# Block-sparse attention and a Fourier mixing layer: copies and the norm's root moved to GpSimd, attention prepared earlier

## The chip, the cores and the metric

The kernel runs on one core of one Trainium2 chip. The metric is the device time of one execution in microseconds (us), lower is better. The kernel is written in Python against the engines: TensorE (PE) for matrix products, VectorE (DVE), ScalarE (ACT), GpSimd (POOL) and SyncE (SP), which only issues DMAs here. Each engine works through its own list of instructions in order and waits at semaphores for the others. GpSimd also issues DMAs, those that convert float32 to float16 on the way.

## The reference

First attention with block selection: q, k, v have the shape (4 batches, 8 heads, 768 positions, 64), float32. Keys form 12 blocks of 64. A query scores each block by its product with the block's mean key, keeps the three best blocks that are not in its future, and its own block. Then the usual softmax attention with a causal mask over the kept blocks:

```python
scores = scale * np.matmul(q, k.transpose(0, 1, 3, 2))
mask = mask & (pos[:, None] >= pos[None, :])
scores = np.where(mask, scores, -1000000000.0)
...
return np.matmul(attn, v)
```

Its result is laid out as x of shape (4, 768, 512), and a Fourier mixing layer with a feed-forward follows:

```python
X = np.fft.fft(x, axis=1)
X = np.fft.fft(X, axis=2)
u = x + np.real(X)
mu = np.mean(u, axis=-1, keepdims=True)
var = np.mean((u - mu) ** 2, axis=-1, keepdims=True)
un = (u - mu) / np.sqrt(var + 1e-06)
out = u + np.maximum(un @ w_ch1, 0.0) @ w_ch2
```

w_ch1 is 512 x 2048, w_ch2 is 2048 x 512.

## The kernel before, in words

The unit of attention is a pair: two heads of one batch, 16 pairs in all, four per batch. A pair P goes through these stages:

- `load` (L160): k and q of both heads by SyncE into float32 tiles (three buffers each); v of pairs 0 to 5 by SyncE into a float32 tile and then a GpSimd cast into one of four float16 v buffers (L171); v of later pairs straight into that buffer by a GpSimd DMA (L164).
- `stage_A` (L186): TensorE transposes k and q into PSUM. VectorE sums k by block (L202) and copies q as float32 (L210). ScalarE copies k of both heads into `qk` (L205), and q of head 0 (L211); VectorE copies q of head 1 (L212).
- `stage_G` (L214): the block scores on TensorE (L220, L223), then on VectorE a transpose (L226), twelve instructions for the top entries (L229), a comparison and a product, and a transpose back into `mt`.
- `stage_K` (L238): GpSimd copies `mt` into the rows 64 to 95 of `qk`, four copies per pair (L241). The score product over 96 rows then adds the block mask by itself.
- `stage_S` (L246), in six parts: scores on TensorE (L260), exponential on ScalarE (L265), and the causal triangle by an `affine_select` on GpSimd (L268), which keeps an element where an affine function of its indices holds.
- `stage_V` (L271): probabilities times v on TensorE (L281), divided by their sum on VectorE into x.

A batch then goes through the mixing layer: folds of x on VectorE (`stage_fold`, `stage_fg`), the transform over positions as matrix products (`stage_Y`, L334, with PSUM copies on ScalarE, L347, and mirrored on VectorE, L349), the transform over features with the residual (`stage_M`, L354: three parts of two row blocks each), the norm in the same function, the feed-forward `stage_W1` (L406) and `stage_W2` (L422).

The norm in `stage_M`: VectorE adds x to the product (u), takes mean and variance (L377, L378), and computes 1/sqrt(var + 1e-6) from an integer seed and two Newton steps (L382 to L391), all as [128,2] instructions. One row block is then normalized on ScalarE (L397), the other on VectorE (L399), and SyncE issues one transposing DMA for each (L403). The feed-forward needs all six.

The order: `attn_slot(i, g, a)` (L483) gives a list of pieces that score pair i, gate pair g, finish pair i-1 and prepare pair a (and load k and q of pair a+3 behind it). Slots 0 to 4 run ahead of everything (L577 to L584). Then, for each batch, the rest of the attention and the batch's mixing layer are woven into one sequence by weights (`weave`, L532). A scheduler lays out each engine's list from that sequence, by its own estimate of when operands are ready; only SyncE's list is kept in exactly the order of the program.

Of the kernel before, what the change touches and what calls it, by code (L numbers as in the profile page):

```python
# [11 lines left out]
FP = mybir.dt.float32  # L12
# [7 lines left out]
S = 768  # L20
# [78 lines left out]
def kernel(  # L99
# [36 lines left out]
    def tt(out, in0, in1, op, eng=None):  # L136
        (eng or nc.vector).tensor_tensor(out=out, in0=in0, in1=in1, op=op)  # L137

    fs_sb = ctile([128, 2, 2, 3, KE], F16, "fs_sb")
    fd_sb = ctile([128, 6, 256], F16, "fd_sb")  # L140
    id32 = ctile([128, 128], FP, "id32")
# [18 lines left out]
    def load(P, who, eng):  # L160
        b, hp = divmod(P, NP)
        src = (q, k, v)[who]
        if who == 2 and P >= NHV:
            nc.gpsimd.dma_start(v_s[P % NVS][:, :, :, 0:64].rearrange("p e st d -> p (e st) d"),  # L164
                                src[b, 2 * hp:2 * hp + 2]
                                .rearrange("e (st p) d -> p (e st) d", p=128))
            return
        if who == 2:
            t = apool.tile([128, 2 * NST, 64], FP, tag="nat2", name=f"nat2_{P}", bufs=2)
            eng.dma_start(t, src[b, 2 * hp:2 * hp + 2].rearrange("e (st p) d -> p (e st) d", p=128))  # L170
            nc.gpsimd.tensor_copy(  # L171
                out=v_s[P % NVS][:, :, :, 0:64].rearrange("p e st d -> p (e st) d"), in_=t)
            return
        if P >= NPAIR:
            return
        t = apool.tile([128, NST, 2, 64], FP, tag=f"nat{who}", name=f"nat{who}_{P}", bufs=3)
        for e in range(2):
            eng.dma_start(t[:, :, e, :],
                          src[b, 2 * hp + e].rearrange("(st p) d -> p st d", p=128))
        nat[P, who] = t  # L180
# [5 lines left out]
    def stage_A(P):  # L186
        d = pairs[P]
        slot = P % NSLOT
        qk = qk_s[slot]
        q32 = apool.tile([128, S], FP, tag="q32", name=f"q32_{P}")  # L190
        d["q32"], d["slot"] = q32, slot
        for who in (1, 0):
            ps = pst([128, NST, 128], f"tp{who}_{P}")
            if 1 <= P <= 3:
                fill(ps.rearrange("p a c -> p (a c)"), 3)
            src = nat[P, who].rearrange("p st e d -> p st (e d)")
            for st in range(NST):
                nc.tensor.transpose(ps[:, st, :], src[:, st, :], id32)  # L198
            flat = ps.rearrange("p a c -> p (a c)")
            if who == 1:  # L200
                kr12 = spool.tile([128, NB], FP, tag="kr12", name=f"kr12_{P}")
                nc.vector.tensor_reduce(out=kr12, in_=flat.rearrange("p (n c) -> p n c", c=64),  # L202
                                        axis=mybir.AxisListType.X, op=ALU.add)
                for e in range(2):
                    nc.scalar.copy(out=qk[0:64, e, 1, :], in_=flat[64 * e:64 * e + 64])  # L205
                tt(kr_s[slot][:, :, 0:NB],
                   kr12.rearrange("p (o n) -> p o n", o=1).to_broadcast([128, 2, NB]), half,
                   ALU.mult)
            else:
                nc.vector.tensor_copy(out=q32, in_=flat)  # L210
                nc.scalar.copy(out=qk[0:64, 0, 0, :], in_=flat[0:64])  # L211
                nc.vector.tensor_copy(out=qk[0:64, 1, 0, :], in_=q32[64:128])  # L212

    def stage_G(P):  # L214
        d = pairs[P]
# [22 lines left out]
    def stage_K(P):  # L238
        mt = pairs[P]["mt"]
        for c in range(4):  # L240
            nc.gpsimd.tensor_copy(  # L241
                out=qk_s[P % NSLOT][64:96, :, 0, 192 * c:192 * c + 192],
                in_=mt[32 * c:32 * c + 32, :].rearrange("p (o x) -> p o x", o=1)
                .to_broadcast([32, 2, 192]))

    def stage_S(P, i):  # L246
        d = pairs[P]
# [106 lines left out]
    def stage_M(b, kp):  # L354
        u_b, x_b = bpool.tile([128, 2, DM], FP, tag="u_b", name=f"u{kp}_{b}", bufs=5), x_t[b]
        u_t[b, kp] = u_b
        mps = pst([128, 2, 512], f"mx{kp}_{b}")
        for k2 in range(2):
            kt = 2 * kp + k2
            sg = 0 if kt < 3 else 1  # L360
            rows = slice(128 * (kt % 3), 128 * (kt % 3 + 1))
            for par in range(2):
                src = ys[b, par][sg]
                o = mps[:, k2, 256 * par:256 * par + 256]
                nc.tensor.matmul(o, src[:, 0, rows], fd_sb[:, 3 * par, :], start=True, stop=False)
                nc.tensor.matmul(o, src[:, 1, rows], fd_sb[:, 3 * par + 1 + sg, :], start=False,
                                 stop=True)
        kk = slice(2 * kp, 2 * kp + 2)
        tt(u_b.rearrange("p k (m two) -> p k two m", two=2),
           mps.rearrange("p k (two m) -> p k two m", two=2),  # L370
           x_b[:, kk, :].rearrange("p k (m two) -> p k two m", two=2), ALU.add)
        if kp == 0:
            un_t[b] = bpool.tile([128, NDT, S], F16, tag="unT", name=f"unT_{b}", bufs=1)
        mv = spool.tile([128, 2, 2], FP, tag="mv", name=f"mv{kp}_{b}")
        for k2 in range(2):
            bst = spool.tile([128, 6], FP, tag="bst", name=f"bst{2 * kp + k2}_{b}", bufs=4)
            nc.vector.bn_stats(out=bst, in_=u_b[:, k2, :])  # L377
            nc.vector.bn_aggr(out=mv[:, k2, :], in_=bst)  # L378
        vr, t2, rs = [spool.tile([128, 2], FP, tag=n, name=f"{n}{kp}_{b}")
                      for n in ("vr", "t2", "rs")]  # L380
        yi = rs.bitcast(I32)
        nc.vector.tensor_scalar(out=vr, in0=mv[:, :, 1], scalar1=1e-6, scalar2=None, op0=ALU.add)  # L382
        nc.vector.tensor_scalar(out=yi, in0=vr.bitcast(I32), scalar1=1, scalar2=None,
                                op0=ALU.arith_shift_right)
        nc.vector.tensor_scalar(out=yi, in0=yi, scalar1=-1, scalar2=0x5f3759df,
                                op0=ALU.mult, op1=ALU.add)
        for _ in range(2):
            nc.vector.scalar_tensor_tensor(out=t2, in0=vr, scalar=-0.5, in1=rs,
                                           op0=ALU.mult, op1=ALU.mult)
            tt(t2, t2, rs, ALU.mult)  # L390
            nc.vector.scalar_tensor_tensor(out=rs, in0=t2, scalar=1.5, in1=rs,  # L391
                                           op0=ALU.add, op1=ALU.mult)
        nb = spool.tile([128, 1], FP, tag="nb", name=f"nb{kp}_{b}")
        nc.vector.tensor_scalar(out=nb, in0=mv[:, 0, 0:1], scalar1=rs[:, 0:1], scalar2=-1.0,  # L394
                                op0=ALU.mult, op1=ALU.mult)
        kt = 2 * kp
        nc.scalar.activation(out=x_b[:, kt, :], in_=u_b[:, 0, :], func=AF.Identity,  # L397
                             scale=rs[:, 0:1], bias=nb)
        nc.vector.tensor_scalar(out=x_b[:, kt + 1, :], in0=u_b[:, 1, :],  # L399
                                scalar1=mv[:, 1, 0:1], scalar2=rs[:, 1:2],  # L400
                                op0=ALU.subtract, op1=ALU.mult)
        for kt in range(2 * kp, 2 * kp + 2):
            nc.sync.dma_start_transpose(un_t[b][:, :, 128 * kt:128 * kt + 128], x_b[:, kt, :])  # L403

# [151 lines left out]
    with tc.manual_schedule(engines={mybir.EngineType.SP}):  # L556
        consts_first()
        kq(2)
        load(0, 2, nc.sync)
        load(1, 2, nc.sync)  # L560
        stage_A(0)
        stage_G(0)
        kq(3)
        stage_A(1)
        stage_K(0)
        stage_G(1)
        kq(4)
        stage_A(2)
        stage_K(1)
        load(2, 2, nc.sync)  # L570
        load(3, 2, nc.sync)
        nc.sync.dma_start(fs_sb, dr["FS"].ap())
        nc.sync.dma_start(fd_sb, dr["FD"].ap())
        for dt in range(NDT):
            load_w1(dt)
        kq(5)
        run(attn_slot(0, 2, 3))  # L577
        run(attn_slot(1, 3, 4))
        load(4, 2, nc.sync)
        run(attn_slot(2, 4, None))  # L580
        load(5, 2, nc.sync)
        run(attn_slot(3, None, 5))
        load(6, 2, nc.sync)
        run(attn_slot(4, 5, None))  # L584
        load(7, 2, nc.sync)
        for b in range(B):
            L = attn_slot(-9, None, 6) if b == 0 else []
            for i in range(NP * (b + 1) + 1, min(NP * (b + 2) + 1, NPAIR + 1)):
                L += attn_slot(i, i + 1, i + 2)
            weave(L, stream(b))  # L590


# [28 lines left out]
```

## Time and profile before

| | |
|---|---|
| median of 3 runs | 377.93 us |
| lowest and highest | 374.62 and 380.5 us |
| the profiled execution | 377.26 us |
| its span, first to last instruction | 375.4 us |
| mean granted TensorE clock | 0.923 of full |
| busy: TensorE, VectorE, ScalarE, GpSimd | 84%, 55%, 47%, 26% |

How to read it: a view of the profile gives an instruction as its start, its duration, its engine, the line of the kernel, what it writes and reads, and in square brackets how long the engine was idle before it and what ended that. "PE" is TensorE's matrix products; a "q" behind an engine's name means its queue (SPq: SyncE's). A clock of 1.00 is 2.4 GHz, 0.50 is 1.2 GHz.

### The profile page before, as it was taken

To read this page: it belongs to the slowest core of one execution; us is meant where nothing else is said; L and a number is where in the kernel's file an instruction comes from. 1 tells how busy PE (TensorE), PEld (TensorE's weight loads), DVE (VectorE), ACT (ScalarE), POOL (GpSimd) and SP (SyncE) were. 2 spreads that over 40 slices of the span, in tenths; PEclk is the share of its full clock that TensorE was granted. 3 is DMA by queue.
4 is the path that set the end of the run, shared out by engine and by line. 5 is a ranking of instruction groups with operands and counts; after the bars stand their busy time and mean duration, and the time that the engine had idled before them with its cause. 6 is when DMAs were issued, how large, how long until landed. Compare 5 with 4: busy or idle time off the path is not lost.

```text
span 375.4 us, 6443 instructions
## 1 busy us (share of the span) xinstructions
PE 316.5 (84%) x2478; PEld 184.6 (49%) x2478; DVE 205.7 (55%) x660; ACT 176.1 (47%) x214; POOL 97.7 (26%) x210
## 2 busy tenths in 40 slices
PE   7788975670599997987879999989999999499995
PEld 3455553350275654563536655653566455156542
DVE  1787678299065639499503738597423179512121
ACT  2478886345158655526546755325575220234200
POOL 3177961641042332311403132300311100000000
PEclk9899898596599999998969999998999999889999
DMA  9999999981615605431990303103300010420012
GB/s 177 211 212 269 201 216 191 210 85 28 141 10 98 87 20 78 86 22 28 141 217 2 21 2 28 50 3 68 130 0 2 2 56 2 84 112 2 0 56 112
DMA packets 94985, 32.45 MB, mean 86 GB/s; under 512 B 88812, under 2 KB 91052, under 8 KB 94956
## 3 DMA queue, kind: packets, MB, share of 16 engines
q1 hardware_dynamic: 74544, 24.98, 30.6%
q0 software_dynamic: 18400, 6.56, 15.7%
q10 hardware_dynamic: 2012, 0.52, 0.7%
q8 instruction: 19, 0.31, 0.3%
q14 instruction: 10, 0.08, 0.1%
HBM read 28.77 MB, written 6.29 MB: 93 GB/s over the span
## 4 chain that ended last, share of the span: by engine, by line
PE 54%; DVE 22%; ACT 10%; issue 5%; DMA 4%; SPq 1%; POOL 1%; ACTq 0%; POOLq 0%; DVEq 0%
PE c L429 15%; PE h L411 13%; PE h L413 7%; PE sc L260 6%; DVE u L137 5%; PE av L281 4%; DVE bst L377 3%; ACT qk L205 3%; ACT pt L265 3%; DMA unT<-x 3%; PE tp L198 2%; DVE kr L202 2%; PE g L220 2%; DMA nat<-in_q_dram 2%; DVE x L137 2%
## 5 line engine op out<-in xcount | busy, mean ns | idle before, releaser
L265 ACT ACTIVATE pt<-sc 128x1024 f16<-128x1024 f32 x96 | 84.6, 919 | 56.6 <-PE sc L260 56.2
L411 PE MATMUL h<-unT,w_sb 128*128 128x512 f16 x256 | 90.7, 398 | 17.4 <-DMA unT<-x 16.3
L429 PE MATMUL c<-w_sb,hT 128*128 128x512 f16 x384 | 89.0, 385 | 4.1 <-DVE x L137 2.1
L268 POOL TENSOR_SCALAR_AFFINE_SELECT pt<-pt 128x256 f16<-128x256 f16 x96 | 40.1, 426 | 149.8 <-ACT pt L265 148.8
L413 PE MATMUL h<-unT,w_sb 128*128 128x256 f16 x256 | 71.7, 283 | 6.7 <-DMA unT<-x 6.7
L420 ACT ACTIVATE hT<-h 128x768 f16<-128x768 f32 x48 | 38.7, 812 | 50.5 <-PE h L413 50.4
L260 PE MATMUL sc<-qk 96*128 96x512 f16 (+3 forms) x256 | 52.7, 316 | 10.3 <-POOL qk L241 3.1
L429 PEld LDWEIGHTS <-hT 128*128 128x128 f16 x384 | 37.5, 99 | 47.1 <-issue 7.7
L411 PEld LDWEIGHTS <-w_sb 128*128 128x128 f16 x256 | 25.8, 101 | 46.4 <-issue 22.5
L418 DVE TENSOR_SCALAR hT<-h 128x768 f16<-128x768 f32 x16 | 15.3, 956 | 59.8 <-PE h L413 59.8
L260 PEld LDWEIGHTS <-qk 96*128 96x128 f16 x256 | 24.0, 100 | 34.6 <-issue 15.1
L241 POOL COPY qk<-mt 32x384 f16<-32x384 f16 x64 | 33.0, 515 | 29.3 <-DVE mt L235 26.6
L205 ACT CAST qk<-tp 64x768 f16<-64x768 f32 x32 | 25.4, 794 | 26.2 <-DVE kr L202 26.0
L413 PEld LDWEIGHTS <-w_sb 128*128 128x128 f16 x256 | 25.9, 101 | 15.4 <-DMA unT<-x 9.2
L137 DVE TENSOR_TENSOR u<-c,u 128x1024 f32<-128x1024 f32 (+1 forms) x13 | 14.8, 1137 | 31.3 <-PE c L429 31.3
L198 PE MATMUL tp<-id,nat 128*128 128x128 f32 x192 | 26.1, 279 | 2.8 <-ACT pt L265 0.9
L281 PEld LDWEIGHTS <-pt 128*128 128x128 f16 x672 | 25.3, 98 | 3.8 <-POOL pt L268 0.8
L281 PE MATMUL av<-v,pt 128*128 128x65 f16 x672 | 26.9, 195 | 0.3 <-POOL pt L268 0.3
L198 PEld LDWEIGHTS tp<-id,nat 128*128 128x128 f32 x192 | 21.7, 143 | 6.8 <-issue 2.7
L226 DVE STREAM_TRANSPOSE gt<-g 128x192 f32<-128x192 f32 x16 | 6.1, 379 | 23.5 <-PE g L223 23.5
L397 ACT ACTIVATE x<-u,nb,rs 128x512 f16<-128x512 f32 x12 | 9.8, 814 | 18.9 <-DVE nb L394 18.9
L347 ACT CAST ty<-yp 128x772 f16<-128x772 f32 x8 | 8.3, 1033 | 19.1 <-PE yp L334 19.1
(73 smaller groups left out, 338.4 us busy)
## 6 DMA issues: line engine op xcount, KB each, us to landing
nat<-in_k_dram SPq DMA_DIRECT2D x32, 192.0 KB, 4.9
nat<-in_q_dram SPq DMA_DIRECT2D x30, 192.0 KB, 4.7
out_dram<-u SPq DMA_DIRECT2D x11, 512.0 KB, 3.0
w_sb<-in_moe_w_ch_dram POOLq DMA_DIRECT2D x8, 512.0 KB, 10.0
nat<-in_v_dram SPq DMA_DIRECT2D x6, 384.0 KB, 12.3
v<-in_v_dram POOLq DMA_DIRECT2D x10, 192.0 KB, 4.9
fs_sb<-c_FS SPq DMA_DIRECT2D x1, 582.0 KB, 5.9
out_dram<-u SPq DMA_DIRECT2D x2, 256.0 KB, 2.0
```

Of the source, the lines that this page charges most:

```text
L137: (eng or nc.vector).tensor_tensor(out=out, in0=in0, in1=in1, op=op)
L198: nc.tensor.transpose(ps[:, st, :], src[:, st, :], id32)
L205: nc.scalar.copy(out=qk[0:64, e, 1, :], in_=flat[64 * e:64 * e + 64])
L241: nc.gpsimd.tensor_copy(out=qk_s[P % NSLOT][64:96, :, 0, 192 * c:192 * c + 192], in_=mt[32 * c:32 * c + 32, :].rearrange("p (o x) -> p o x ...
L260: nc.tensor.matmul(ps[:, co:co + q1 - q0], qk[0:96, e, 1, 128 * jt:128 * jt + 128], qk[0:96, e, 0, q0:q1], start=True, stop=True)
L265: nc.scalar.activation(out=pt[:, o:o + wid], in_=ps, func=AF.Exp, scale=0.125)
L268: nc.gpsimd.affine_select(out=dg, in_=dg, pattern=[[0, 2], [1, 128]], base=0, channel_multiplier=-1, compare_op=ALU.is_ge, fill=0.0)
L281: nc.tensor.matmul(av[:, e, 66 * st:66 * st + 65], pt[:, co:co + 128], vv[:, e, jt, 0:65], start=(cnt == 0), stop=(cnt == 20))
L411: nc.tensor.matmul(hp[:, 0:512], w1s, unT[:, dt, 0:512], start=(dt == 0), stop=(dt == NDT - 1))
L413: nc.tensor.matmul(hp[:, 512:768], w1s, unT[:, dt, 512:768], start=(dt == 0), stop=(dt == NDT - 1))
L420: nc.scalar.activation(out=hT, in_=hp, func=AF.Relu)
L429: nc.tensor.matmul(cps[:, part, :], h_t[b, it][:, 128 * st:128 * (st + 1)], w2_sb[:, it, :], start=(it == 0), stop=(it == NIT - 1))
```

## The change

GpSimd gets a helper `pcopy`, an `affine_select` whose condition holds everywhere, so that it copies. It is used for v's casts, for the mask copies, and for the q copies of both heads, which read the float32 copy of q and leave ScalarE and VectorE. In the norm the seed stays on VectorE; the Newton steps and the bias go to GpSimd as ten [128,2] instructions, and both row blocks are normalized on ScalarE. In the order, pairs 5 and 6 are prepared and gated one slot earlier each, so that both are done ahead of the first FFT, and the first weave starts without pair 6.

```diff
+    def pcopy(out, in_, n):
+        nc.gpsimd.affine_select(out=out, in_=in_, pattern=[[0, i] for i in n], base=0,
+                                channel_multiplier=0, compare_op=ALU.is_ge, fill=0.0)
...
-            nc.gpsimd.tensor_copy(
-                out=v_s[P % NVS][:, :, :, 0:64].rearrange("p e st d -> p (e st) d"), in_=t)
+            pcopy(v_s[P % NVS][:, :, :, 0:64].rearrange("p e st d -> p (e st) d"), t,
+                  [2 * NST, 64])
...
                 nc.vector.tensor_copy(out=q32, in_=flat)
-                nc.scalar.copy(out=qk[0:64, 0, 0, :], in_=flat[0:64])
-                nc.vector.tensor_copy(out=qk[0:64, 1, 0, :], in_=q32[64:128])
+                for e in range(2):
+                    pcopy(qk[0:64, e, 0, :], q32[64 * e:64 * e + 64], [S])
...
         for c in range(4):
-            nc.gpsimd.tensor_copy(
-                out=qk_s[P % NSLOT][64:96, :, 0, 192 * c:192 * c + 192],
-                in_=mt[32 * c:32 * c + 32, :].rearrange("p (o x) -> p o x", o=1)
-                .to_broadcast([32, 2, 192]))
+            pcopy(qk_s[P % NSLOT][64:96, :, 0, 192 * c:192 * c + 192],
+                  mt[32 * c:32 * c + 32, :].rearrange("p (o x) -> p o x", o=1)
+                  .to_broadcast([32, 2, 192]), [2, 192])
...
+        nb = spool.tile([128, 2], FP, tag="nb", name=f"nb{kp}_{b}")
         yi = rs.bitcast(I32)
+        po = nc.gpsimd
...
         for _ in range(2):
-            nc.vector.scalar_tensor_tensor(out=t2, in0=vr, scalar=-0.5, in1=rs,
-                                           op0=ALU.mult, op1=ALU.mult)
-            tt(t2, t2, rs, ALU.mult)
-            nc.vector.scalar_tensor_tensor(out=rs, in0=t2, scalar=1.5, in1=rs,
-                                           op0=ALU.add, op1=ALU.mult)
-        nb = spool.tile([128, 1], FP, tag="nb", name=f"nb{kp}_{b}")
-        nc.vector.tensor_scalar(out=nb, in0=mv[:, 0, 0:1], scalar1=rs[:, 0:1], scalar2=-1.0,
-                                op0=ALU.mult, op1=ALU.mult)
-        kt = 2 * kp
-        nc.scalar.activation(out=x_b[:, kt, :], in_=u_b[:, 0, :], func=AF.Identity,
-                             scale=rs[:, 0:1], bias=nb)
-        nc.vector.tensor_scalar(out=x_b[:, kt + 1, :], in0=u_b[:, 1, :],
-                                scalar1=mv[:, 1, 0:1], scalar2=rs[:, 1:2],
-                                op0=ALU.subtract, op1=ALU.mult)
+            tt(t2, vr, rs, ALU.mult, po)
+            tt(t2, t2, rs, ALU.mult, po)
+            po.tensor_scalar(out=t2, in0=t2, scalar1=-0.5, scalar2=1.5, op0=ALU.mult, op1=ALU.add)
+            tt(rs, rs, t2, ALU.mult, po)
+        tt(nb, mv[:, :, 0], rs, ALU.mult, po)
+        po.tensor_scalar(out=nb, in0=nb, scalar1=-1.0, scalar2=None, op0=ALU.mult)
+        for k2 in range(2):
+            nc.scalar.activation(out=x_b[:, 2 * kp + k2, :], in_=u_b[:, k2, :],
+                                 func=AF.Identity, scale=rs[:, k2:k2 + 1], bias=nb[:, k2:k2 + 1])
...
-        run(attn_slot(2, 4, None))
+        run(attn_slot(2, 4, 5))
         load(5, 2, nc.sync)
-        run(attn_slot(3, None, 5))
+        run(attn_slot(3, 5, 6))
         load(6, 2, nc.sync)
-        run(attn_slot(4, 5, None))
+        run(attn_slot(4, 6, None))
         load(7, 2, nc.sync)
         for b in range(B):
-            L = attn_slot(-9, None, 6) if b == 0 else []
+            L = []
             for i in range(NP * (b + 1) + 1, min(NP * (b + 2) + 1, NPAIR + 1)):
-                L += attn_slot(i, i + 1, i + 2)
+                L += attn_slot(i, *((None, 7) if i == 5 else (i + 1, i + 2)))
```

## Rows read from the trace of the kernel before

**Rows 1.** Stretches: length, busy PE, PEld, DVE, ACT, POOL, clock, DMA share, GB/s.
```profile
17.00:56.20 39.20, 33.27 (x364) 21.43 (x358) 29.28 (x109) 31.29 (x39) 31.05 (x65) 0.96 1.14 224
...
59.90:63.10 3.20, 0.00 (x0) 0.00 (x0) 3.17 (x9) 2.15 (x3) 0.00 (x0) 0.90 1.25 199
...
68.60:71.70 3.10, 0.00 (x1) 0.00 (x1) 1.17 (x2) 1.03 (x1) 2.33 (x4) 0.50 1.20 201
...
85.70:96.50 10.80, 0.00 (x0) 0.00 (x0) 7.46 (x32) 4.94 (x6) 0.41 (x1) 0.53 0.19 37
```

**Rows 2.** Waits: engine line, waited for: us in total, times, longest.
```profile
PE sc L260 <- POOL qk L241: 3.1, 1, 3.1
```

**Rows 3.** Timeline of TensorE, SyncE and VectorE, second and fourth norm.
```profile
189.93 0.40 PE L413 MATMUL h<-unT,w_sb 128*128 128x256 f16 x1 [4.03 <-DMA unT<-x]
...
174.85 5.85 SPq L403 DMA_TRANSPOSE unT<-x  x4
...
326.45 1.86 PE L411 MATMUL h<-unT,w_sb 128*128 128x512 f16 x4 [5.45 <-DMA unT<-x]
...
316.41 0.16 DVE L385 TENSOR_SCALAR rs<-rs 128x2 int32<-128x2 int32 x1
...
320.01 7.75 SPq L403 DMA_TRANSPOSE unT<-x  x6
```

**Rows 4.** One line's instructions: count, duration ns min/median/max, first and last start.
```profile
L241 POOL COPY qk<-mt x64: 497/502/822, 17.1 to 269.1; 32x384 f16<-32x384 f16 x64
...
L268 POOL TENSOR_SCALAR_AFFINE_SELECT pt<-pt x96: 398/408/726, 25.7 to 296.9; 128x256 f16<-128x256 f16 x96
...
L171 POOL CAST v<-nat x6: 819/823/824, 19.7 to 69.2; 128x768 f16<-128x768 f32 x6
...
L440 POOL CAST w_sb<-nat x4: 177/178/182, 49.3 to 49.7; 1x1 f16<-1x1 f32 x4
...
L137 DVE TENSOR_TENSOR lt<-gt,mx x16: 347/358/908, 14.9 to 265.7; 128x192 f16<-128x192 f32 x16
```

**Rows 5.** Timeline of GpSimd, to the first norm.
```profile
17.13 2.46 POOL L241 COPY qk<-mt 32x384 f16<-32x384 f16 x4 [13.22 <-DVE mt L235]
19.66 0.82 POOL L171 CAST v<-nat 128x768 f16<-128x768 f32 x1
...
64.65 0.82 POOL L171 CAST v<-nat 128x768 f16<-128x768 f32 x1 [8.45 <-DMA nat<-in_v_dram]
...
69.17 0.82 POOL L171 CAST v<-nat 128x768 f16<-128x768 f32 x1 [2.63 <-DMA nat<-in_v_dram]
```

**Rows 6.** Timeline of VectorE and TensorE around the first FFT.
```profile
59.93 0.95 DVE L202 TENSOR_REDUCE kr<-tp 128x12 f32<-128x768 f32 x1
...
69.69 1.01 DVE L349 CAST tr<-yp 128x768 f16<-128x768 f32 x1 [0.93 <-ACT ty L347]
...
72.64 0.42 PE L365 MATMUL mx<-fd_sb,ty 128*128 128x256 f16 x1
```

**Rows 7.** The chain that ended last, 75.4 to 93.4 us by line, then single pieces.
```profile
by line: DVE bst L377 19.8%; DVE u L137 19.3%; DVE x L399 5.1%; DVE x L137 4.8%; DVE q L210 4.8%; DVE mx L229 4.8%; DVE kr L202 4.8%; ACT x L397 4.6%; DVE t L388 4.4%; DVE t L137 3.3%; DVE qk L212 3.1%; DVE rs L391 3.0%; DVE sd L137 2.9%; D
...
75.48 1.23 DVE u L137
...
92.07 0.17 DVE t L388
...
92.91 0.82 ACT x L397
...
96.68 2.42 DMA unT<-x
```

**Rows 8.** VectorE's busy time in that stretch: all, and on the gate tile.
```profile
75.48:93.34 17.86, 17.68 (x72) 0.79 0.53 55
...
75.48:93.34 17.86, 2.09 (x14) 0.79 0.53 55
```

**Rows 9.** Timeline of VectorE: a product beside a cast of GpSimd.
```profile
19.78 0.91 DVE L137 TENSOR_TENSOR lt<-gt,mx 128x192 f16<-128x192 f32 x1
```

## The prediction

> **What bounds the kernel now.** I read the shares of the whole span first; they say little, since the stages have different limits. The table of stretches shows where TensorE stands still, and the worst lies around the first FFT: nothing in 59.9 to 63.1 us, nothing in 68.6 to 71.7, nothing in 85.7 to 96.5, the granted clock at half (1.2 GHz) in the last two [rows 1]. The list of waits names what ended the second of them: a score product held 3.1 us on a mask that GpSimd copies [rows 2]; the third ends with the transposed norm. Later two places are left: TensorE waits 4.03 us for the norm of the second batch and 5.45 us for that of the fourth [rows 3]. The change touches all of these through the norm, and the first also through the order of the attention. Everywhere else behind 104 us TensorE is nearly full, and relief of another engine there is counted at nothing.
>
> **GpSimd before the first FFT.** From 17.0 to 56.2 us, the attention of pairs 0 to 4, GpSimd is busy for 31.05 of 39.2 us, idle for 8.15 [rows 1]. The change puts into that stretch:
> - q head copies, two selects of 768 columns per pair. Pair 0's fall into the 13.22 us in which GpSimd waits for its first mask [rows 5]. Pairs 1 to 6 stay: 12 selects. No row shows one of 768 float columns. GpSimd's copies take 502 ns at 384 columns and 822 at 768; their line gives 395 at 256, and the select of 256 columns takes 408 (medians) [rows 4]. So I put the select on the copies' line, 3% up, 0.86 us at 768. Below, with a larger fixed part, it could be 0.7. Above, with no fixed part at all, 408/256 = 1.59 ns a column, 1.22 us. I take 0.86, from the nearest rows: 12 x 0.86 = 10.3 us.
> - Masks and v casts as selects: on that line no change; at the upper end 0.61 us per mask and 1.22 per cast.
> - Pair 5's four masks, before at 70 us: 4 x 0.5 = 2.0.
>
> 31.05 + 10.3 + 2.0 = 43.4 us of work in 39.2: the masking of pair 3's probabilities, and with it the last AV product of the first batch, comes 4.2 us later. ScalarE there gives up three q copies and takes over pair 6's two k copies, VectorE gives up its q head copies; neither ends the stretch any more, so both count as nothing.
>
> **From there to the first norm.** The fold had pair 6's reduction and q copy in its midst (0.95 us at 59.93, the copy as long, overlapping: 1.8 in all) [rows 6]; they go ahead now. So the FFT starts 4.2 - 1.8 = 2.4 us later. Its second product waited from 70.7 (last mirrored copy) to 72.64 us [rows 6], because pair 5's scores stood in front and their masks stood on GpSimd behind the v cast of 69.17 us [rows 5]. With pair 5 prepared earlier that wait is gone, and so are pair 6's gate products among the FFT's matmuls. Start 70.7 + 2.4 = 73.1; eight matmuls of 256 columns at 1.2 GHz, 0.21 us each, 1.7: the first residual add at 74.8 instead of 75.48 [rows 7]. GpSimd's overload is thus paid for by the stalls that it replaces.
>
> **The first norm.** From 75.48 to 93.34 us, its last norm write, VectorE is busy for 17.68 of 17.86 us [rows 8]. By the chain's shares of 18.0 us [rows 7] it loses: three norms' Newton steps (4.4, 3.3 and 3.0%: 1.9 us), their second halves (5.1%: 0.9) and the bias, cut off in that list (some 0.5): 3.3 us; pair 7's head copy (3.1%: 0.6); pair 6's gating, 2.09 us busy for 14 instructions [rows 8], 2.0 with its overlaps and the last transpose. 17.9 - 5.9 = 12.0, so the last seed of the root is there at 86.8. Then ten dependent [128,2] instructions on GpSimd. No row shows one: on VectorE a step that nothing overlaps takes 0.17 us and some 0.02 of issue [rows 7], GpSimd's 1x1 casts take 0.18, a select of 256 columns 0.41 [rows 4]. I take 0.2, the size of the first two, with 0.12 (casts that overlap) and 0.4 as ends: 2.0 us, with a hop 88.9. Both halves follow each other on ScalarE, 2 x 0.82: 90.5. Last transpose issued 1.2 us later, landed after 2.42 [rows 7]: 94.1 instead of 99.1, a gain of 5.0. Scores of pair 6 that the order now puts ahead of the feed-forward fill a little of the hole; counted at nothing.
>
> One thing works against this. A VectorE product of two SBUF operands, 358 ns as a rule, took 908 at 19.78 us [rows 4, 9], while GpSimd ran a v cast from 19.66 to 20.48 [rows 5]. Pair 7's q selects are two instructions of that length beside the norm; I charge one such hold, 0.5 us. First batch: -4.5 us. The Trainium skill ("SBUF — State Buffer", section "Who interferes with whom") says that such a product and a reading GpSimd instruction share a port pair under an exclusive lock, and the later one stands for the whole instruction; the trace agrees with its 0.91 beside 0.36 us. By that rule both of pair 7's selects could hold VectorE for their whole length, 1.7 us instead of 0.5, and the sum below would be 371.0.
>
> **The later norms.** Second batch: SyncE starts its transposes at 174.85 us, when the first half norm is there, then issues k and q loads, then the last two transposes [rows 3]. VectorE loses about 1.1 us per norm and ScalarE a q copy; GpSimd's 2 us come in. I put the first half 2.5 us earlier, and as SyncE's order is rigid, the landing too: -2.5 of the 4.03 us (ends 0 and -4). Third batch: no wait for the norm, 0. Fourth: the seed of the first root is there at 316.5; GpSimd done at 318.5, the first half at 319.3, so SyncE's six transposes (7.75 us from 320.01) start 0.7 us earlier [rows 3]. Three roots on GpSimd end at 322.5, the last halves at 324.1, in time for SyncE: -0.5 us.
>
> **Sum.** The profiled execution took 377.26 us (span 375.4 and 1.9 around it); the median of the runs shown, 377.93, lies 0.7 above. 377.3 - 4.5 - 2.5 - 0.5 = 369.8 us, 2.2% under the median. About 2% is what a measurement of this kernel can tell from no change.
>
> **Rivals.**
> - *GpSimd is dear per instruction* (slower). At the upper ends, 1.22 us per q select and 0.4 per small instruction, the stretch to 56.2 us gets 14.6 (q), 2.2 + 2.4 (20 masks 0.11 dearer, four new ones) and 1.6 (four casts): 51.9 us of work, 12.7 late instead of 4.2. The first norm lands at 94.1 + 8.5 + 2.0 + 0.5 = 105.1, 6.0 late; three roots in series (12 us from 316.5) put the last halves of the fourth batch at 330.1 and the landing 4 us late; the second batch gains 0.5. 377.3 + 9.5 = 386.8. It decides at 44% of the way, a q select of 1.02 us and a small instruction of 0.29. For it: a GpSimd that was 79% busy has little to give. Against: the 256-column select lies on the copies' line.
> - *Only the roots are dear.* Selects as forecast, small instructions 0.38 us: +1.8 in the first batch, +1.8 in the second, +3.9 in the fourth: 377.3. For it: the root is a chain in which nothing overlaps. Against: the casts at 0.18. The Trainium skill ("GPSIMD Engine Reference", section "Engine selection") sends two-input elementwise work to VectorE, as about twice as fast; no row of before has such a pair, and twice VectorE's 0.19 us, an estimate from that page, would be this rival's price.
> - *GpSimd is not the bound of the attention.* If probabilities are masked ahead of later pairs' q copies, the 8.15 idle us take the new work: no delay, 365.6. For it: that idle time exists. Against: an engine runs its list in order.
> - *v's cast holds the roots.* Pair 8's k and q loads (four of 197 KB, 3.9 us at the 201 GB/s of [rows 1]) stand ahead of pair 5's v now. It lands at 73 or, with pair 9's too, 77 us; GpSimd stands until then, with selects of pairs 5 and 7 behind: +2, 371.8. For it: GpSimd stood 8.45 and 2.63 us for just these casts [rows 5]. Against: the last root isn't due before 86.
>
> **How the numbers follow.** Forecast 0.45 (its own range 365 to 374.5), GpSimd dear 0.17, roots dear 0.15, GpSimd not the bound 0.13, v's cast 0.10. The range 363 to 383 leaves out two thirds of the dear case and the far tail of the fast one. Under 370.4 us lie a good half of the forecast (0.24), 0.13 and 0.02: 0.39. Over 385.5 lie over half of the dear case and a little for an order that I don't foresee: 0.12. The rest, 0.49, is within 2%.
>
> **What would show it.** Right: GpSimd over 90% busy from 17 to 60 us, selects of 768 columns near 0.86 us, the last AV product of the first batch near 61, no wait of TensorE on a mask copy, the first residual add near 75, the first feed-forward running from 94, the wait before the second under 2 us. Wrong: q selects over 1.02 us, root instructions 0.29 us or more apart, or the first feed-forward starting behind 99 us.

## The result and the profile after

The changed kernel took 363.44 us (median of 4 runs, 362.66 to 366.35) beside 379.15 us for the kernel before (four runs, the three of the table above and one more), a ratio of 0.967 (95% interval 0.958 to 0.977). A later repeat, measured with six runs of it and 17 of the kernel before, gave 363.58 beside 378.7: 0.959 (0.955 to 0.964). Runs over 1.5% above the fastest of the same kernel are left out of every ratio, so a ratio isn't quite the quotient of the two medians. It is faster by 3.3 and 4.1%, where 2.2 was forecast: at the low edge of the forecast range of 363 to 383, and below 365 to 374.5, the range of the forecast's own mechanism. The profiled execution took 366.35 us, its span is 364.6.

The head of the page after (busy time, share of the span, number of instructions):

```profile
PE 315.6 (87%) x2478; PEld 186.1 (51%) x2478; DVE 192.4 (53%) x548; ACT 173.1 (47%) x210; POOL 150.3 (41%) x362
```

GpSimd went from 26 to 41% busy. What it got, from the groups of instructions by shape (count, busy us, mean ns, idle before):

```profile
L140 POOL TENSOR_SCALAR_AFFINE_SELECT qk<-mt 32x384 f16<-32x384 f16 x64 | 33.1, 517 | 12.7 <-DVE mt L239 9.6
L140 POOL TENSOR_SCALAR_AFFINE_SELECT qk<-q 64x768 f16<-64x768 f32 x32 | 27.5, 859 | 23.8 <-DVE q L214 22.8
...
L140 POOL TENSOR_SCALAR_AFFINE_SELECT v<-nat 128x768 f16<-128x768 f32 x6 | 5.5, 924 | 0.1
...
L137 POOL TENSOR_TENSOR t<-vr,rs 128x2 f32<-128x2 f32 x24 | 4.8, 200 | 30.9 <-DVE vr L387 25.0 <-DVE mv L381 4.9
```

A q select takes 0.859 us, the forecast's 0.86. The mask selects stand at 517 ns beside copies of 502 [rows 4], the v casts at 924 beside 823. The idle time ahead of the casts, in which GpSimd waited for v [rows 5], is down to 0.1 us.

Stretches of the changed kernel (columns as in [rows 1]): the attention before the first FFT, the first mixing layer up to its feed-forward, the first feed-forward, and the second one:

```profile
17.00:56.20 39.20, 31.35 (x302) 20.10 (x303) 26.84 (x102) 25.64 (x31) 33.56 (x65) 0.91 1.10 216
70.42:96.03 25.61, 16.43 (x139) 10.77 (x140) 19.64 (x53) 12.62 (x15) 15.85 (x45) 0.70 0.79 109
...
96.03:130.94 34.91, 34.28 (x298) 22.33 (x298) 15.24 (x49) 24.13 (x30) 14.83 (x29) 0.94 0.55 88
...
180.21:209.71 29.50, 29.49 (x256) 18.44 (x254) 14.56 (x50) 20.56 (x26) 12.51 (x24) 1.00 0.44 75
```

The last two of these in the kernel before:

```profile
96.56:135.90 39.34, 36.14 (x310) 22.19 (x311) 18.43 (x67) 24.97 (x32) 11.81 (x24) 0.91 0.47 78
...
185.30:222.14 36.84, 32.48 (x256) 19.34 (x254) 15.68 (x52) 22.15 (x28) 9.18 (x20) 0.91 0.50 70
```

Three things stand in these rows. GpSimd is 33.56/39.2 = 86% busy ahead of the first FFT (87% from 17 to 60 us), not over 90%. The first feed-forward starts at 96.03, hardly earlier than the 96.56 of before, but is 4.4 us shorter, with 12 TensorE products fewer in it. The second one is 7.3 us shorter with the same 256 products: TensorE no longer stands still in it [rows 3], and its clock is granted in full.

To compare all kernels I cut each span at the same four points, the first TensorE instruction of each kind: the first FFT's first product, the first feed-forward's first (W1), the second FFT's, the third FFT's. Lengths in us, each from one profiled execution; two profiles of the changed kernel (its own and the repeat) differ by 0.9 us or less in each column but the last, where it is 1.1. The names in brackets are those of the runs below:

| kernel | to FFT 1 | FFT 1 to W1 | W1 to FFT 2 | FFT 2 to FFT 3 | rest |
|---|---|---|---|---|---|
| before | 63.1 | 33.4 | 58.7 | 82.9 | 137.3 |
| after | 70.4 | 25.6 | 52.3 | 77.3 | 139.0 |
| only the order (p_order) | 69.0 | 25.9 | 53.5 | 81.8 | 138.3 |
| only the q selects (p_q) | 64.8 | 27.8 | 58.6 | 76.4 | 138.3 |
| only the norm (p_norm) | 60.7 | 36.2 | 58.6 | 80.8 | 140.1 |
| all but the order (m_order) | 62.4 | 26.5 | 56.3 | 76.6 | 138.0 |
| all but the q selects (m_q) | 68.6 | 24.9 | 55.4 | 81.3 | 140.3 |
| all but the norm (m_norm) | 70.9 | 25.5 | 52.1 | 81.3 | 137.2 |

A profiled execution can lie some us off its kernel's median, so a difference of one or two us in a column shows little: that of m_order took 361.49 us (median 363.74), that of the changed kernel 366.35 (363.44), that of p_q 367.83 (370.37).

After minus before: +7.3, -7.8, -6.4, -5.6, +1.7: -10.8 us, the difference of the two spans. The forecast, cut in the same way: +2.4, -6.9, 0, -2.5, -0.5. (The first two are its -4.5.) The forecast's own mark, the landing of the last normalized block, shows in the first product of 256 columns in the feed-forward, which reads that block. TensorE after:

```profile
96.03 0.58 PE L411 MATMUL h<-unT,w_sb 128*128 128x512 f16 x1 [3.41 <-DMA unT<-x]
...
101.17 0.28 PE L413 MATMUL h<-unT,w_sb 128*128 128x256 f16 x1 [0.63 <-DMA unT<-x]
```

and before:

```profile
96.56 0.58 PE L411 MATMUL h<-unT,w_sb 128*128 128x512 f16 x1 [10.87 <-DMA unT<-x]
...
99.14 0.39 PE L413 MATMUL h<-unT,w_sb 128*128 128x256 f16 x1 [1.89 <-DMA unT<-x]
```

The first norm thus ends at 101.2, 2 us later than before, where 94.1 was forecast. Yet TensorE stands still for 3.4 us ahead of the feed-forward and not 10.9, since it has attention to do meanwhile.

### The profile page after: what moved, and what is told of

Read it like the earlier page. It is cut to its first block, busy times and chain, and to the rows that moved or that the text cites. A ratio compares the mean times of both kernels' runs of the same rounds, so it can differ in the third digit from the quotient of the medians.

```text
span 364.6 us, 6505 instructions
## 1 busy us (share of the span) xinstructions
PE 315.6 (87%) x2478; PEld 186.1 (51%) x2478; DVE 192.4 (53%) x548; ACT 173.1 (47%) x210; POOL 150.3 (41%) x362
## 4 chain that ended last, share of the span: by engine, by line
PE 59%; DVE 15%; POOL 10%; ACT 7%; issue 5%; DMA 3%; SPq 0%; ACTq 0%; POOLq 0%; DVEq 0%
PE c L429 16%; PE h L411 15%; PE h L413 8%; PE sc L263 6%; PE av L284 4%; DVE u L137 3%; PE tp L202 3%; PE yp L337 3%; POOL qk L140 2%; DVE bst L380 2%; ACT pt L268 2%; DMA nat<-in_q_dram 2%; ACT x L400 2%; POOL t L137 2%; PE g L224 2%
## 5 line engine op out<-in xcount | busy, mean ns | idle before, releaser
L411 PE MATMUL h<-unT,w_sb 128*128 128x512 f16 x256 | 89.6, 394 | 9.2 <-DMA unT<-x 9.2
L271 POOL TENSOR_SCALAR_AFFINE_SELECT pt<-pt 128x256 f16<-128x256 f16 x96 | 40.9, 436 | 78.9 <-ACT pt L268 77.8
L413 PE MATMUL h<-unT,w_sb 128*128 128x256 f16 x256 | 70.5, 279 | 1.4 <-DMA unT<-x 1.4
L418 DVE TENSOR_SCALAR hT<-h 128x768 f16<-128x768 f32 x16 | 15.3, 955 | 56.3 <-PE h L413 56.3
L411 PEld LDWEIGHTS <-w_sb 128*128 128x128 f16 x256 | 25.6, 100 | 37.2 <-issue 12.6
L140 POOL TENSOR_SCALAR_AFFINE_SELECT qk<-mt 32x384 f16<-32x384 f16 x64 | 33.1, 517 | 12.7 <-DVE mt L239 9.6
L140 POOL TENSOR_SCALAR_AFFINE_SELECT qk<-q 64x768 f16<-64x768 f32 x32 | 27.5, 859 | 23.8 <-DVE q L214 22.8
L284 PE MATMUL av<-v,pt 128*128 128x65 f16 x672 | 28.4, 198 | 3.8 <-POOL pt L271 3.8
L400 ACT ACTIVATE x<-u,nb,rs 128x512 f16<-128x512 f32 x24 | 18.2, 805 | 28.2 <-POOL nb L398 28.2
L284 PEld LDWEIGHTS <-pt 128*128 128x128 f16 x672 | 26.5, 101 | 9.0 <-POOL pt L271 4.7
L413 PEld LDWEIGHTS <-w_sb 128*128 128x128 f16 x256 | 25.6, 100 | 7.3 <-DMA unT<-x 2.8
L202 PEld LDWEIGHTS tp<-id,nat 128*128 128x128 f32 x192 | 22.5, 147 | 7.3 <-issue 3.3
```

The source lines that it names most:

```text
L140: nc.gpsimd.affine_select(out=out, in_=in_, pattern=[[0, i] for i in n], base=0, channel_multiplier=0, compare_op=ALU.is_ge, fill=0.0)
L271: nc.gpsimd.affine_select(out=dg, in_=dg, pattern=[[0, 2], [1, 128]], base=0, channel_multiplier=-1, compare_op=ALU.is_ge, fill=0.0)
L284: nc.tensor.matmul(av[:, e, 66 * st:66 * st + 65], pt[:, co:co + 128], vv[:, e, jt, 0:65], start=(cnt == 0), stop=(cnt == 20))
L400: nc.scalar.activation(out=x_b[:, 2 * kp + k2, :], in_=u_b[:, k2, :], func=AF.Identity, scale=rs[:, k2:k2 + 1], bias=nb[:, k2:k2 + 1])
L411: nc.tensor.matmul(hp[:, 0:512], w1s, unT[:, dt, 0:512], start=(dt == 0), stop=(dt == NDT - 1))
L413: nc.tensor.matmul(hp[:, 512:768], w1s, unT[:, dt, 512:768], start=(dt == 0), stop=(dt == NDT - 1))
```

## The experiments

**One part taken back at a time.** Order, q copies, norm and the other selects, each as before and the rest as changed:

```diff
# m_order
-        run(attn_slot(2, 4, 5))
+        run(attn_slot(2, 4, None))
...
# m_q
-                for e in range(2):
-                    pcopy(qk[0:64, e, 0, :], q32[64 * e:64 * e + 64], [S])
+                nc.scalar.copy(out=qk[0:64, 0, 0, :], in_=flat[0:64])
+                nc.vector.tensor_copy(out=qk[0:64, 1, 0, :], in_=q32[64:128])
# m_norm
-            tt(t2, vr, rs, ALU.mult, po)
+            nc.vector.scalar_tensor_tensor(out=t2, in0=vr, scalar=-0.5, in1=rs,
+                                           op0=ALU.mult, op1=ALU.mult)
...
# m_sel
-            pcopy(v_s[P % NVS][:, :, :, 0:64].rearrange("p e st d -> p (e st) d"), t,
-                  [2 * NST, 64])
+            nc.gpsimd.tensor_copy(
+                out=v_s[P % NVS][:, :, :, 0:64].rearrange("p e st d -> p (e st) d"), in_=t)
...
```

> The changed kernel with the order of before (pairs 5 and 6 prepared and gated as late as before); the moved copies and the moved norm stay. Theory A (the attention prepared ahead carries the gain: it fills TensorE's holes before the first feed-forward and leaves less for the stages behind it): most of the gain goes, 373 to 377 us, and the first feed-forward's stage is about 4 us longer again. Theory B (the load taken off ScalarE and VectorE carries it, order is a detail): 364 to 367 us, stages behind the first feed-forward as in the changed kernel.

Measured: 363.74 us, 0.958 (0.953 to 0.962), as theory B has it. By the medians the order taken back costs nothing. The first FFT starts at 62.4 with all of GpSimd's new work in place, so with the old order that work does not delay it.

> The changed kernel with the q head copies back on ScalarE and VectorE, all else as changed. Theory A: the q copies only cost, since GpSimd is full before the first FFT: first FFT about 65 instead of 70.4 us, total 358 to 361. Theory B: ScalarE's freed 12.7 us shorten the stages behind 96 us; with the copies back the total is 367 to 371, though the first FFT starts earlier.

Measured: 369.94 us, 0.976 (0.972 to 0.980), the total of theory B. The q copies are the part whose loss hurts most, 6.4 us above the changed kernel, and the first FFT is late without them too (68.6).

> The changed kernel with the whole norm as before (Newton steps on VectorE, one half on VectorE). By my forecast's terms the norm is worth some 3.5 us in the first batch, 2.5 in the second and 0.5 in the fourth: 370 to 372 us. Theory A: about 366, since the holes that the norm leaves are filled by attention. Theory B: 370 to 373, with the wait before the second feed-forward back at some 4 us.

Measured: 366.73 us, 0.966 (0.960 to 0.972), 3.2 us above, though the intervals touch. From the first FFT to its feed-forward it needs 25.5 us with the old norm, no more than the 25.6 with the new one: the loss isn't there but in the second batch (81.3 for 77.3), where TensorE stands still for the norm:

```profile
183.12 0.40 PE L416 MATMUL h<-unT,w_sb 128*128 128x256 f16 x1 [6.24 <-DMA unT<-x]
```

> The changed kernel with v's casts and the mask copies as plain copies again; the q copies stay selects. A select of 384 or 768 columns takes what a copy takes, so both theories: 362 to 365 us, no difference that can be measured. A third view, that the selects are what makes GpSimd fast enough: 367 or more.

Measured: 362.84 us, 0.955 (0.952 to 0.959). Whether masks and v casts are selects or plain copies makes no difference that can be told.

**One part alone, on the kernel before.** The edits are the same parts of the diff, now added to the kernel before.

> The kernel before with nothing but the two q head copies moved to GpSimd selects. If the parts add up (q copies 6.5 us, norm 3.3, order 0): 372 to 375, and its feed-forward stages of the first two batches shorter. If the q copies pay only together with the norm: 377 to 380, as before. Its first FFT near 62 us, as with the order of before and all else changed (62.4).

Measured: 370.37 us, 0.974 (0.966 to 0.981), a larger gain than either expectation. In its profile the second batch gets its whole gain from this part alone (76.4). That execution, 367.83 us, is the fastest of four that reach to 373.26; for the others it isn't shown.

> The kernel before with nothing but the moved norm (Newton steps and bias on GpSimd, both halves on ScalarE). Taken away from the changed kernel it cost 3.3 us, added to the kernel with the moved q copies and the old order it seems to give 6.6 (370.4 to 363.7). If the norm pays by itself (VectorE's list ahead of the first two feed-forwards is shorter whatever ScalarE does): 373 to 377. If it needs the q copies gone from ScalarE, since it puts three more half norms there: 378 to 381.

Measured: 377.32 us, 0.994 (0.991 to 0.998), between the two expectations. The first product of 256 columns stands at 101.43, 40.7 us after the first FFT, where the kernel before has 36.0. But the profile doesn't put this loss down to the norm. GpSimd stood 15.83 us for a v that landed late (8.45 before [rows 5]), the masks came behind that cast, and a score product waited 8.79 us for them (3.1 before [rows 2]). GpSimd and TensorE of this run:

```profile
69.59 0.82 POOL L171 CAST v<-nat 128x768 f16<-128x768 f32 x1 [15.83 <-DMA nat<-in_v_dram]
```

```profile
74.01 1.14 PE L260 MATMUL sc<-qk 96*128 96x512 f16 x3 [8.79 <-POOL qk L241]
```

SyncE issued this load of v at 50.73 us, before at 41.62, both long ahead of the first root, which starts at 81.56. So what the new norm alone is worth in the first batch can't be read from this run.

> The kernel before with nothing but the earlier preparation of pairs 5 and 6. In the changed kernel the order moved the first FFT by 8 us and gave it back behind it, sum 0. If that holds alone: 378 to 382, first FFT at 67 to 70 us. If filling the hole of the old norm (10.8 us of TensorE) makes it worth more here: 373 to 377.

Measured: 370.8 us, 0.978 (0.973 to 0.984), a larger gain than either expectation. It makes the first FFT late (69.0) and gains more behind it.

The wait in the second batch, with only the order (TensorE; start, duration, in brackets the idle time before and what ended it), and with only the q selects:

```profile
178.63 0.60 PE L411 MATMUL h<-unT,w_sb 128*128 128x512 f16 x2
183.33 0.39 PE L413 MATMUL h<-unT,w_sb 128*128 128x256 f16 x1 [4.10 <-DMA unT<-x]
```

```profile
181.91 0.59 PE L415 MATMUL h<-unT,w_sb 128*128 128x512 f16 x2
182.94 0.28 PE L417 MATMUL h<-unT,w_sb 128*128 128x256 f16 x1 [0.44 <-DMA unT<-x]
```

SyncE issues the last two transposes of this norm, in both kernels behind the first four and the next loads of k and q:

```profile
176.43 2.81 SPq L403 DMA_TRANSPOSE unT<-x  x2
```

```profile
178.86 2.51 SPq L407 DMA_TRANSPOSE unT<-x  x2
```

Counted from the second FFT (at 148.40 and 151.15), the last issue ends after 30.8 and 30.2 us, almost alike; the wait ends after 34.9 and 31.8. So the 3 us lie mostly between issue and landing. There the load of the DMA engines (their share column) is 1.52 in the one, from 174 to 186 us, and 1.04 in the other, from 176 to 188. Which transfer stood in front wasn't settled.

**Which q copy, and why.** Two variants of the changed kernel leave head 1 to GpSimd and give head 0 back to ScalarE, once from PSUM as before (x_ps), once from the float32 copy in SBUF (x_sb). Each has one of the two marked lines:

```diff
-                for e in range(2):
-                    pcopy(qk[0:64, e, 0, :], q32[64 * e:64 * e + 64], [S])
+                nc.scalar.copy(out=qk[0:64, 0, 0, :], in_=flat[0:64])   # x_ps
+                nc.scalar.copy(out=qk[0:64, 0, 0, :], in_=q32[0:64])    # x_sb
+                pcopy(qk[0:64, 1, 0, :], q32[64:128], [S])
```

> As the run before, but ScalarE copies head 0 from PSUM, as in the kernel before; head 1 stays on GpSimd. Theory 1 (ScalarE's time): 367 to 370, as the run before. Theory 2 (the PSUM tile held): 367 to 370, and the run before near 363. Theory 3 (VectorE's copy): 362 to 365, both.

Measured: 369.8 us, 0.971 (0.967 to 0.976), the same as with both copies back. So VectorE's copy of head 1 costs nothing that can be told, and ScalarE's copy of head 0 is the whole loss of some 6 us.

> The changed kernel, but ScalarE copies head 0 of q from the float32 copy in SBUF; head 1 stays a select on GpSimd. ScalarE has its load of before, and the PSUM tile of q is still free after VectorE's copy. Undoing both q copies cost 6.5 us (369.9 against 363.4). Theory 1 (ScalarE's 0.79 us per pair, behind which exponentials and the feed-forward's PSUM evacuations queue): 367 to 370. Theory 2 (the PSUM tile of the transposed q, held until ScalarE came to its copy, kept TensorE waiting): 362 to 365. Theory 3 (VectorE's copy of head 1): 362 to 365.

Measured: 366.54 us, 0.963 (0.956 to 0.970), between the two theories. The copies themselves are alike, 792 ns from PSUM and 829 from SBUF (medians). The waits of TensorE, 96 to 255 us, with the copy from PSUM (engine, line, waited for: us in total, times, longest):

```profile
PE sc L263 <- ACT qk L209: 3.6, 2, 2.1
PE sc L263 <- ACT qk L215: 3.3, 2, 2.7
```

L215 is the q copy, and a score product waits for it up to 2.7 us, in the second batch. With the copy from SBUF no wait names it. Behind 103 us the two variants have the same list on each engine, instruction for instruction, so there they differ in nothing but what this copy reads: what TensorE waits for is the PSUM tile that the copy holds. The copy comes late since it stands in ScalarE's list behind two half norms (of 1.52 us together, from 164.52). In the stretch from FFT 2 to FFT 3, x_ps, x_sb and the changed kernel need 80.1, 77.9 and 77.3 us. So the hold of the PSUM tile is most of the loss in that batch. Elsewhere it is less certain. Ahead of the first FFT x_ps is 2.5 us behind x_sb (70.1 and 67.6), but there the scheduler also put instructions at other places. And x_sb's 3 us over the changed kernel, which would be ScalarE's time, aren't shown: its profile is no longer (span 364.1 beside 364.6 and 363.9), and the intervals overlap.

**Can the parts be chosen better?** The norm moved in the first batches only, in the order of before, with all selects:

```diff
-        for _ in range(2):
-            tt(t2, vr, rs, ALU.mult, po)
...
+        if b == 1:      # c_n1;  "if b < 2:" in c_n2
+            for _ in range(2):
+                tt(t2, vr, rs, ALU.mult, po)
...
+        else:
+            for _ in range(2):
+                nc.vector.scalar_tensor_tensor(out=t2, in0=vr, scalar=-0.5, in1=rs,
+                                               op0=ALU.mult, op1=ALU.mult)
...
```

> A combination: the order of before, q copies, masks and casts as selects, and the norm moved in the second batch alone. By the profiles the moved norm shortens only the second batch (65.4 to 61.4 us from its FFT to the end of its first feed-forward product), leaves the first alone and lengthens the third and fourth by 0.8 and 1.0: 361 to 363 us. If the first batch's norm needs the move after all when the order is that of before: 365 or more.

Measured: 366.18 us, 0.965 (0.958 to 0.971): no gain, as the second expectation has it.

> A combination: order of before, q copies, masks and casts as selects, the norm moved in the first two batches and left on VectorE in the last two. With the norm moved in the second batch only, the first batch's feed-forward took 39.6 instead of 37.7 us, so it needs the move too; in the third and fourth batch the profiles show the moved norm 0.8 to 1.0 us behind: 361 to 363 us, 1 to 2 under the changed kernel. If the difference in the later batches was only the clock of those profiles: 363 to 364.5, the same.

Measured: 364.7 us, 0.961 (0.957 to 0.966). The rest behind its third FFT is 136.5 us, 2.5 under that of the changed kernel (1.5 under the repeat's), but the time as a whole isn't lower.

> The changed kernel itself, beside the other three on one chip, for their comparison and for a second profile of its stages: 362.5 to 365 us.

Measured: 363.58 us, as above. No combination was shown to beat the changed kernel; m_sel, m_order and c_n2 can't be told from it.

**The parts don't add up.** Alone, order, q selects and norm are worth 2.2% (interval 1.6 to 2.7), 2.7% (1.9 to 3.4) and 0.6% (0.2 to 1.0), 5.4 together, where the whole change is worth 3.3 to 4.1: somewhat more than the intervals allow. Taken from the whole they are worth 0, 6.4 and 3.2 us, or 0, 1.7 and 0.8%. Order and q selects close the same gap behind the first FFT: 25.9 and 27.8 us, each alone, of 33.4, and both together 25.6.

## Why the prediction was right and where it wasn't

The sign and the range were right. The sum came within 2% by luck: errors of opposite sign met in it. Beside the forecast, the way to the first FFT is 4.9 us longer, the two stretches behind it 0.9 and 6.4 shorter, the second batch 3.1 shorter, the rest 2.2 longer.

*The price of the selects: right.* 0.859 us for 0.86. The rival in which GpSimd is dear fell by its own point of decision, 1.02 us.

*The delay before the first FFT: size and cause wrong.* The step that failed is "neither ends the stretch any more, so both count as nothing", said of ScalarE and VectorE, beside the 4.2 us charged to GpSimd. The FFT starts at 70.4, not 65.5. GpSimd's selects move it by -0.8 us (m_order, beside before) to +1.9 (after, beside m_q); the new order alone by +5.8. The delay lies ahead of the last AV product of the first batch, forecast near 61 us: it starts at 56.09 before, at 63.48 with only the order, at 64.33 after the change. From its end to the FFT the three need 6.3, 4.7 and 5.3 us. The chain that ended last with only the order (p_order), in five of its pieces (start, us, what), shows what stands in front of it:

```profile
56.24 0.88 DVE kr L202
...
57.13 0.79 ACT qk L205
...
57.94 0.80 ACT qk L205
...
59.84 0.74 PE g L220 x8
...
63.64 0.65 PE av L281 x21
```

These are pair 6's reduction, its two k copies and its block scores, which came behind the FFT or into the fold before. From 17 us to the FFT, TensorE waits 4.9 us for ScalarE's k copies in this run, 2.2 in the kernel before. In the changed kernel VectorE's list also has pair 6's gating ahead of the second half of the fold:

```profile
62.96 0.98 DVE mx L233 x12
...
67.83 1.54 DVE zw L137 x2
```

That gating ends 0.6 us after the last AV product does (65.72 and 65.13); with only the order VectorE stands 0.86 us for that product. So the work of pairs 5 and 6 on TensorE, ScalarE and VectorE together carries the delay, and the shares of the three weren't separated. The forecast moved this work out of the later chain, rightly, and forgot to put it where it went. The masking that it charged to GpSimd is there: in the changed kernel AV products wait 3.6 us for GpSimd's masks of the probabilities ahead of the first FFT, 0.3 in the whole kernel before. But m_order has 2.6 us of such waits too, and its FFT isn't late.

*FFT to first feed-forward: size right, cause wrong.* The forecast had 33.4 - 6.9 = 26.5 us here; it is 25.6. Of the 5.9 us that it took off VectorE's chain it put 3.3 to the norm, but the old norm does as well: with it (m_norm) the last block is read 30.0 us after the first FFT (100.9 - 70.9), without a wait, with the new one 30.7, and 36.0 before. SyncE's last transpose is issued 27.1 us after the FFT with the old norm, 29.5 with the new. The order alone gives 29.9, the q selects alone 31.9. So what shortened it is the rest: pair 6's work and the copies off VectorE's list, and the waits on mask copies (3.1 us before, none after). How much each of these brings wasn't separated. The norm brings nothing here; GpSimd's list shows two reasons:

```profile
91.99 0.82 POOL L140 TENSOR_SCALAR_AFFINE_SELECT qk<-q 64x768 f16<-64x768 f32 x1
92.79 0.19 POOL L137 TENSOR_TENSOR t<-vr,rs 128x2 f32<-128x2 f32 x1
93.06 0.85 POOL L140 TENSOR_SCALAR_AFFINE_SELECT qk<-q 64x768 f16<-64x768 f32 x1
93.99 0.20 POOL L137 TENSOR_TENSOR t<-t,rs 128x2 f32<-128x2 f32 x1
94.27 0.19 POOL L395 TENSOR_SCALAR t<-t 128x2 f32<-128x2 f32 x1
...
96.22 0.21 POOL L398 TENSOR_SCALAR nb<-nb 128x2 f32<-128x2 f32 x1
```

The ten small instructions are 0.20 us long, as forecast, but start 0.27 to 0.28 us apart: 2.8 us, not 2.0 (mis-sized; the rivals with dear roots decided at 0.29 and had 0.38 to 0.4). And the third root shares its engine with pair 7's q selects and the causal triangles: its seed is there at 90.49, its bias at 96.43, 5.9 us later. In that time GpSimd ran two q selects and a triangle, and stood 0.99 us for the exponential that this triangle needs. The forecast charged these selects to VectorE, 0.5 us, not to the root queued with them. The other misses, the first residual add at 78.55 instead of 74.8 and 4.9 of the landing's 7.1 us, come with the late FFT.

*"Everywhere else behind 104 us ... counted at nothing": wrong by 6.4 us.* So was "fill a little of the hole; counted at nothing", said of the scores that the order puts ahead of the feed-forward. More of the next batch's attention is done before the first feed-forward begins, so less is woven into it. It is the order that does it: from W1 to FFT 2 the kernels with the new order need 52.1 to 55.4 us, those with the old one 56.3 to 58.7. The score tile's rows (TensorE's and ScalarE's work on it), up to W1 and in W1, in the kernel before and after:

```profile
0.00:96.56 96.56, 23.19 (x114) 30.54 (x35) 0.84 1.02 178
96.56:135.90 39.34, 7.99 (x38) 11.97 (x14) 0.91 0.47 78
```

```profile
0.00:96.03 96.03, 27.19 (x122) 33.45 (x38) 0.86 1.02 179
96.03:130.94 34.91, 6.68 (x32) 10.81 (x12) 0.94 0.55 88
```

Of the 4.4 us by which this feed-forward is shorter, 1.9 are less work (TensorE is busy for 36.14 and 34.28 us) and 2.6 less standing. A late FFT is thus not simply lost time: what TensorE does while it is late is missing from the full stretch behind. Added to the kernel before, the order costs 5.8 us ahead of the FFT and gives back 7.5 and 5.2 in the two stretches behind. In the changed kernel it costs 8.0 (62.4 to 70.4) and gives back 0.9 and 4.0 by the profiles, though all of it by the medians. The two profiled executions lie 4.9 us apart, the medians 0.3, so where the rest comes back isn't shown.

*Second batch: mechanism right, term mis-sized.* -5.6 instead of -2.5. SyncE starts the transposes 17.1 us after the second FFT (165.34 - 148.29), before 19.6: 2.5 us earlier, as forecast. Every kernel with the new norm in this batch has 17.0 to 17.5 there, every one with the old norm 19.2 to 19.6. The first product of 256 columns comes 32.1 us after that FFT instead of 34.7, so 2.5 us earlier, too. The other 3.1 us lie behind it. The forecast took the 4.03 us of the wait as all that could be had (ends 0 and -4). The stretches of the kernel before around that wait show what it missed:

```profile
185.30:189.93 4.63, 0.60 (x4) 0.10 (x2) 3.08 (x7) 1.59 (x2) 0.39 (x1) 0.87 2.06 206
189.93:194.00 4.07, 4.07 (x14) 1.99 (x15) 0.00 (x0) 1.49 (x2) 0.00 (x0) 0.50 1.22 309
```

After standing for 4.03 us TensorE runs on at a granted clock of 0.50 (1.2 GHz); its products keep the longer duration to about 195.5, some 5.5 us, of which half, 2.8, is lost. 4.03 + 2.8 = 6.8 of the 7.3 us by which this feed-forward is shorter after; against that it starts 1.9 us later after its FFT (31.9 for 30.0).

Nor does the norm bring it alone: in the new order it takes both the norm and the q selects (81.3 without the one or the other), for two different reasons. Without the new norm TensorE waits for the norm, the 6.24 us shown above. With it but without the q selects TensorE doesn't wait for the norm; ahead of the feed-forward a score product waits for ScalarE's q copy instead. That wait from the second FFT to its feed-forward, in the kernel before, in p_norm and in m_q:

```profile
PE sc L260 <- ACT qk L211: 0.2, 1, 0.2
...
PE sc L260 <- ACT qk L211: 3.1, 1, 3.1
...
PE sc L263 <- ACT qk L215: 3.0, 1, 3.0
```

In the old order the profile of p_q shows the whole gain with the q selects alone; there the last transposes land sooner after their issue, by a cause that stays open.

*Third and fourth batch: 0 and -0.5 forecast, +1.7 measured (+0.7 in the repeat's profile).* The rest is 136.5 to 138.3 us in the six kernels with the old norm there, 138.0 to 139.1 in the four with the new one and q selects for both heads, 140.1 to 140.4 in the four where ScalarE does the norm and a q copy. So a norm that ScalarE does beside a q copy is a loss of 2 to 3 us here; without the q copy it is one of about 1 us, which is within what two profiles of one kernel differ by. In the fourth batch SyncE's six transposes start 15.2 us after the FFT's first product (308.38 - 293.22), before 14.9, where 0.7 earlier was forecast.

*Rivals.* "v's cast holds the roots" fell: GpSimd's idle time for v went to 0.1 us. In p_norm a wait for v holds the masks instead, and TensorE with them for 8.79 us. "GpSimd is not the bound of the attention" was half right, since the selects hardly move the first FFT though masks do wait behind them; its 365.6 us is nearest to the result, though by a sum that shares the wrong credit to the norm.

## What to carry to other kernels

When work is moved ahead of a stage, charge it at its new place on every engine it uses, and count as gain what is no longer woven into the full stretch behind; a stage that starts late with more work done has lost less than its delay. The wait of TensorE in the full stretch of the second batch was worth its length and half of the slow-clock time behind it (4.03 and 2.8 us). And an engine's copy of 0.8 us can cost more than its own duration if it reads a PSUM tile into which TensorE's next product is to go and stands late in its engine's list: move it, or let it read an SBUF copy. Read a part's worth from its profile with care: in p_norm the loss came from a v that landed late, not from the part that was added.

## What the runs showed of the hardware that wasn't expected

- Small GpSimd instructions that follow each other, [128,2], are 0.20 us long and start 0.27 to 0.28 us apart; VectorE's take 0.17 with some 0.02 of issue [rows 7].
- VectorE slows beside GpSimd more often than charged. The fold's two products take 1.03 us in the kernel before (554 ns each), and 2.01 us here beside two q selects, which are longer, too. VectorE and GpSimd of the changed kernel:

```profile
60.63 2.01 DVE L137 TENSOR_TENSOR zw<-sd 128x768 f16<-128x768 f16 x2
```

```profile
61.40 1.92 POOL L140 TENSOR_SCALAR_AFFINE_SELECT qk<-q 64x768 f16<-64x768 f32 x2
```

  The Trainium skill ("SBUF — State Buffer", section "Who interferes with whom") describes such a hold; the trace agrees, with this 2.01 beside 1.03 us.
